# A fused RWKV-attention and squared-ReLU kernel: one written-out order of all work exchanged for another

## The chip, the cores and the metric

The kernel runs on one core of one Trainium2 chip. The metric is the device time of one execution in microseconds (us); lower is better. Five engines work side by side, each in its own order: PE (TensorE, matrix products), DVE (VectorE), ACT (ScalarE), POOL (GpSimd) and SP, which here only issues DMAs.

## What is computed

Four inputs r, k, v, w of shape 4 x 8 x 768 x 48 (batch, heads, time, head size) go through a recurrent attention with a state of 48 x 48 per head; its result y, laid out as 3072 tokens of 384, goes through a two-layer network with a squared ReLU.

```python
for t in range(S):
    cur = np.einsum('bhd,bhe->bhde', u[None] * kt, vt)
    y[:, :, t] = np.einsum('bhd,bhde->bhe', rt, state + cur)
    state = wt[:, :, :, None] * state + np.einsum('bhd,bhe->bhde', kt, vt)
x = y.transpose(0, 2, 1, 3).reshape(B * S, H * D)
h = x @ w_in            # 3072 x 384 @ 384 x 2048
r = np.maximum(h, 0.0)
return (r * r) @ w_out  # 2048 x 384
```

## The kernel before

The 3072 tokens are cut into 12 steps of 256 (4 batches of 3 steps). In a step two neighbouring times share a partition, so that every tile has 128 partitions. A step runs through these operations, each a small function named after its word in the order:

- Loads (`load_step`, L209): w, k, r, v of a step, 384 KB each. `load_wi` (L219) and `load_wo` (L224) load the two weights in four pieces of 768 KB into the staging tiles `w_st`; `cast` (L229) makes fp16 of them into `wi_sb` and `wo_sb`, on the engine that the word names.
- Decay: `ww_` (w·w, L295), `lw_` (its logarithm on ACT, L299), `cum_` (cumulative sums as products with triangular constants on PE, L337), `exp_` and `ac_` (ACT, L356 and L360), `rd_` (DVE, L369: r and k times their decay into `rdec_buf`).
- `tr_` and `rkt_` (L379, L387) transpose them on PE into `rkT_b` in the first three steps; later ones use a transposing DMA, `dtr_` (L392).
- `p_` (PE, L400) makes the scores, `pm_` (DVE, L413) masks them, `su_`, `ts_`, `sn_` (PE, mostly DVE, mostly POOL) carry the state S on.
- The term with u: `load_u` and `ub_` (L239, L243) spread the row u over all partitions with a product of PE, `uc_` copies it to `u_bc`; `ku_`, `qp_`, `q_`, `vq_` (L315 to L328) are k·u, its product with r, the sum of it over a head, and that times v.
- `y_`, `yq_`, `yc_`, `yb_`, `yd_` (PE, L465 to L502) add up y in a PSUM tile `att`; `ysb_` copies it as `y_sb_b`; `yt_` with `xt_`, or a transposing DMA `dyt_` (L527), turn it into `xT_b`.
- The network: `m1_` (L532) is one eighth of x @ w_in, six products of 128 x 256; `rl_` (relu, L541) and `sq_` (square, L549) make `gt_b`. `m2_` (L557) is a quarter of the second product for 128 tokens, four products; from step 5 on seven half-width products `pw_` (L601), with sums `tw_`, `sw_`, `cx_`, `ow_` around them, do its work. `store` (L637) writes the result.

`warm_` (L641) is a dummy: n products of 128 x 512 on a tile of zeros, whose result nobody reads. PE has two double tiles `att` and four single tiles `one`, which all of this takes in turns.

The order of everything is written out by hand in the table `ORDER` (L17 to L94): one word for each operation, in program order. A word names the operation, the step and the part; `:n` gives the PSUM tile, and `=A`, `=V` or `=G` the engine (ACT, DVE, POOL). A loop at L659 issues the words one after the other, so each engine gets its instructions in the order of the words that fall to it, and waits are placed where the data ask for them. Nothing reorders them later.

Of the kernel before, what the change touches and what calls it, by code (L numbers as in the profile page):

```python
# [22 lines left out]
tr_.1.0:0 y_.0:0 ld.2.k ld.2.r rkt_.1.1=V rkt_.1.0=V cast.i.0=A yq_.0 yc_.0 ysb_.0.0=V yd_.0 su_.1:1 ysb_.0.1=V
p_.1.1:m yt_.0.0:1 ku_.1=G sn_.0.1=G xt_.0.0=V yt_.0.1:0 qp_.1=G pm_.1.1 xt_.0.1=A cast.i.1=A p_.1.0:0 pm_.1.0
m1_.0.0:0 m1_.0.1:3 rl_.0.1=A rl_.0.0=A q_.1 ts_.1.0=V ww_.2=G sn_.1.0=G m1_.0.4:2 m1_.0.5:1 m1_.0.3:3 rl_.0.3=A
vq_.1=V lw_.2 rl_.0.5=V ts_.1.1=V m1_.0.2:0 ld.2.v y_.1:0 rl_.0.2=A cast.i.3=V ld.3.w yc_.1 yq_.1 yd_.1 ysb_.1=A
rl_.0.4=A ld.0.o ld.1.o cum_.2:1 m1_.0.7:0 exp_.2 rl_.0.7=A yt_.1:1 ku_.2=V ld.3.k rw_.2=G xt_.1=V m1_.0.6:2 kw_.2=V
sq_.0.0=V m1_.1.6:3 m1_.1.5:1 m1_.1.3:0 v_.2=A rl_.1.6=A rl_.1.5=A rl_.1.3=A m1_.1.0:3 rd_.2.0 ld.2.o ld.3.o rd_.2.1
rl_.0.6=V m1_.1.2:1 qp_.2=V m1_.1.1:0 sq_.0.1=A rl_.1.1=V rl_.1.2=A ac_.2 rl_.1.0=A ww_.3=G sq_.1.0=A m1_.1.7:2
tr_.2.0:1 cast.o.0=G su_.2:0 tr_.2.1:0 rkt_.2.0=V rkt_.2.1=V m1_.1.4:3 sn_.1.1=G ts_.2.0=V cast.o.1=G m2_.1.1.0:1  # L30
p_.2.0:0 ld.3.r p_.2.1:1 q_.2 pm_.2.0 rl_.1.4=A sn_.2.0=G vq_.2=G m2_.1.0.0:3 rl_.1.7=A m2_.0.0.0:2 m2_.0.1.0:0
pm_.2.1 m2_.0.1.1 m2_.0.0.1 ld.4.r yc_.2:1 yq_.2 cast.o.2=V kw_.3=V sq_.1.3=A ld.4.w sq_.0.3=A sq_.1.1=A lw_.3
cum_.3:0 sq_.0.2=A m2_.1.0.1 m2_.1.1.1 sq_.1.2=V ku_.3=V exp_.3 cast.o.3=A ld.4.k rw_.3=V m2_.0.0.2 m2_.0.1.2
m2_.1.1.2 m2_.1.0.2 m2_.0.1.3 qp_.3=V rd_.3.1 y_.2 ww_.4=G ld.3.v tw_.3=V rd_.3.0 yb_.2 m2_.1.1.3 m2_.0.0.3 os_.0.1=A
ysb_.2=A yt_.2:0 q_.3 m2_.1.0.3 lw_.4 dtr_.3.1 os_.1.1=A cum_.4:1 dtr_.3.0 xt_.2=V os_.0.0=A m1_.2.2:1 rw_.4=G
os_.1.0=A exp_.4 kw_.4=V ac_.4 ld.5.w rl_.2.2=A ku_.4=V qp_.4=G m1_.2.3:2 m1_.2.1:3 v_.3=A ac_.3 rl_.2.3=A rd_.4.1
vq_.3=G rl_.2.1=A rd_.4.0 ld.4.v m1_.2.0:0 ld.5.k ld.5.v m1_.2.6:1 rl_.2.0=V p_.3.0:0 ld.5.r rl_.2.6=A su_.3:1
# [663 lines left out]
```

## Time and profile before

| | us |
|---|---|
| three runs | 179.57, 179.72, 180.99; median 179.72 |
| profiled execution, its own time | 181.33 |
| its span, first to last instruction | 179.6 |
| busy: PE, DVE, ACT, POOL | 170.3, 150.6, 125.7, 113.9 |
| first product with w_in (L538) starts | 21.33 |
| last product of the result ends, about | 176.2 |

Times in rows of the profile are microseconds from the span's start, if not marked ns. A row of the timeline has start, duration, engine, line, operation, out<-in and how often (x8 are eight of them); what stands in brackets is how long the engine was idle just before, and what ended that wait. In a group of instructions stand, behind the bar, the busy time, the mean duration of one in ns, and the idle time before them. A busy share is an average over stages: what a change is worth is read from the stage and from the wait that ends last there. Matrix products are pipelined and overlap in the records, so eight of them in a row are better read by the time of all eight.

### The profile page before, as it was taken

The numbers are of one execution on the slowest core, as the hardware profiler recorded it, in microseconds if no ns is written. First come the engines' busy times: TensorE is split into PE (matmuls) and PEld (weight loads), VectorE is DVE, ScalarE is ACT, GpSimd is POOL, SyncE is SP. The second block draws the span as 40 slices with busy tenths as digits, with TensorE's granted clock in tenths as the row PEclk, the third lists the DMA queues.
The fourth block names the chain that finished last, engine by engine and source line by source line (L and its number), as shares of the span: only waits on it lengthen the run. The fifth ranks groups of instructions, "written<-read, shape, count | busy, mean of one in ns | idle before, by whom it ended". The sixth has DMA issues, their size and how long they took to land.

```text
span 179.6 us, 6485 instructions
## 1 busy us (share of the span) xinstructions
PE 170.3 (95%) x2771; PEld 134.3 (75%) x2771; DVE 150.6 (84%) x238; ACT 125.7 (70%) x209; POOL 113.9 (63%) x109
## 2 busy tenths in 40 slices
PE   7898799999999999998998999999999899999993
PEld 2274687856686777586875888888988788989992
DVE  5559899999689679999798999988899777768752
ACT  5368569897599667589675988688794777575510
POOL 6289944370575498155796399398989792392430
PEclk9999999999999999999999999999999999999999
DMA  5999999998999979799999959999989031040042
GB/s 153 324 353 377 350 253 350 271 309 229 228 260 243 268 192 236 151 303 133 275 185 300 227 130 262 135 183 271 235 221 157 4 91 36 12 175 0 4 173 92
DMA packets 82670, 36.59 MB, mean 204 GB/s; under 512 B 75857, under 2 KB 81106, under 8 KB 82642
## 3 DMA queue, kind: packets, MB, share of 16 engines
q1 hardware_dynamic: 82642, 36.19, 81.8%
q8 instruction: 21, 0.34, 0.8%
q14 instruction: 7, 0.06, 0.1%
HBM read 25.17 MB, written 4.72 MB: 166 GB/s over the span
## 4 chain that ended last, share of the span: by engine, by line
PE 79%; DVE 8%; DMA 5%; issue 3%; ACT 3%; DVEq 0%; ACTq 0%
PE one L538 31%; PE one L615 16%; PE one L561 12%; PE att L460 7%; DMA xT_b<-y_sb_b 3%; PE att L410 3%; PE att L433 2%; DMA w_b<-in_w_dram 2%; DVE pmT_b L421 2%; PE one L385 2%; PE one L643 1%; PE att L343 1%; ACT gt_b L545 1%; PE one L245 1%; ACT att L358 1%
## 5 line engine op out<-in xcount | busy, mean ns | idle before, releaser
L538 PE MATMUL one<-xT_b,wi_sb 128*128 128x256 bf16 x576 | 70.0, 273 | 1.3 <-ACT gt_b L545 0.7
L538 PEld LDWEIGHTS <-wi_sb 128*128 128x128 f16 x576 | 55.0, 98 | 10.0 <-issue 1.4
L545 ACT ACTIVATE gt_b<-one 128x512 f16<-128x512 f32 x71 | 41.0, 596 | 14.7 <-PE one L538 11.4
L553 ACT ACTIVATE gt_b<-gt_b 128x1024 bf16<-128x1024 f16 x39 | 40.3, 1052 | 1.7 <-DVE gt_b L547 1.4
L421 DVE TENSOR_TENSOR pmT_b<-att,mask 128x1024 bf16<-128x1024 f32 x22 | 26.7, 1219 | 3.0 <-PE att L410 2.8
L561 PE MATMUL one<-wo_sb,gt_b 128*128 128x384 f16 x160 | 28.7, 326 | 0.0
L615 PEld LDWEIGHTS <-gt_b 128*128 128x128 bf16 x280 | 23.3, 98 | 0.6
L561 PEld LDWEIGHTS <-gt_b 128*128 128x128 bf16 x160 | 15.0, 98 | 9.3
L547 DVE TENSOR_SCALAR gt_b<-one 128x512 f16<-128x512 f32 x25 | 16.9, 686 | 4.0 <-PE one L538 3.7
L321 POOL TENSOR_TENSOR ku_b<-ku_b,r_b 128x768 f32<-128x768 f32 x8 | 14.5, 1817 | 4.6 <-DVE ku_b L316 4.5
L327 POOL TENSOR_TENSOR vq_b<-v_b,q_b 128x768 bf16<-128x768 f32 x10 | 15.4, 1545 | 1.5 <-DVE q_b L324 0.9
L615 PE MATMUL one<-wo_sb,gt_b 128*128 128x192 f16 x168 | 16.3, 246 | 0.0
L447 POOL TENSOR_TENSOR S_b<-t_b,ac_buf 128x192 bf16<-128x192 f32 x17 | 9.2, 544 | 10.8 <-DVE t_b L443 7.1
L297 POOL TENSOR_TENSOR ww_b<-w_b 128x384 f32<-128x384 f32 x10 | 11.1, 1107 | 6.3 <-DMA w_b<-in_w_dram 6.3
L313 POOL TENSOR_TENSOR k_b<-k_b,w_b 128x384 f32<-128x384 f32 x8 | 9.1, 1132 | 7.6 <-DMA k_b<-in_k_dram 7.6
L316 POOL TENSOR_TENSOR ku_b<-k_b,u_bc 128x768 f32<-128x768 f32 x6 | 11.1, 1846 | 2.9 <-ACT u_bc L249 2.9
L510 ACT CAST y_sb_b<-att 128x768 bf16<-128x768 f32 x11 | 8.8, 799 | 5.3 <-PE att L460 4.8
L376 DVE TENSOR_TENSOR rdec_buf<-r_b,att 128x768 bf16<-128x768 f32 (+1 forms) x13 | 11.4, 886 | 0.9 <-ACT ac_buf L363 0.7
L376 DVE TENSOR_TENSOR rdec_buf<-k_b,att 128x768 bf16<-128x768 f32 (+1 forms) x13 | 11.5, 886 | 0.7 <-ACT ac_buf L363 0.3
L615 PE MATMUL one<-w_st_b,gt_b 128*128 128x192 f16 x112 | 11.4, 246 | 0.0
L324 DVE TENSOR_REDUCE q_b<-ku_b 128x16 f32<-128x768 f32 x12 | 11.3, 944 | 0.0
L358 ACT ACTIVATE att<-att 128x768 f32<-128x768 f32 x12 | 9.6, 801 | 2.1 <-PE att L345 1.9
(107 smaller groups left out, 287.1 us busy)
## 6 DMA issues: line engine op xcount, KB each, us to landing
w_b<-in_w_dram SPq DMA_DIRECT2D x12, 384.0 KB, 4.7
k_b<-in_k_dram SPq DMA_DIRECT2D x12, 384.0 KB, 4.9
r_b<-in_r_dram SPq DMA_DIRECT2D x12, 384.0 KB, 6.0
v_b<-in_v_dram SPq DMA_DIRECT2D x12, 384.0 KB, 4.8
out_dram<-w_st_b SPq DMA_DIRECT2D x23, 192.0 KB, 2.1
w_st_b<-in_moe_w_in_dram SPq DMA_DIRECT2D x4, 768.0 KB, 6.8
w_st_b<-in_moe_w_out_dram SPq DMA_DIRECT2D x4, 768.0 KB, 9.5
rkT_b<-rdec_buf SPq DMA_TRANSPOSE x18, 3.5
```

What stands on the lines that cost most here:

```text
L321: product("qp_", s)(ku[:], ku[:], buf("r", s)[:, :, 0:2, :])
L327: product("vq_", s)(buf("vq", s)[:].rearrange("p j h d -> p h j d"), buf("v", s)[:], buf("q", s)[:, :, :, None].to_broadcast([C, H, 2, D]))
L358: nc.scalar.activation(cs[:, :, 0:DM], cs[:, :, 0:DM], AF.Exp)
L376: nc.vector.tensor_mul(rdec[:, i, :, heads, 0:D], x.rearrange("p h j d -> p j h d"), decay[:, None, :, :].to_broadcast([C, 2, n, D]))
L421: nc.vector.tensor_mul(pmT, ps_p[:].rearrange("p e (a x) -> p (e a) x", a=2), mk.to_broadcast([C, 4, 2 * C]))
L460: nc.tensor.matmul(ps_y[rows, c, cols], lhsT, rhs, start=fresh, stop=True, skip_group_check=True)
L538: nc.tensor.matmul(ps1[:, j, :], wi_sb[:, n // 4, kk, n % 4 * 128:(n % 4 + 1) * 128], xT[:, :, kk, :], start=(kk == 0), stop=(kk == KT - 1))
L545: nc.scalar.activation(rl, m1, AF.Relu, scale=RS)
L547: nc.vector.tensor_scalar(out=rl, in0=m1, scalar1=RS, scalar2=0.0, op0=ALU.mult, op1=ALU.max)
L553: nc.scalar.activation(gt, rl, AF.Square)
L561: nc.tensor.matmul(m2, gt[:, n, c * C:(c + 1) * C], wo_sb[:, n, :], start=(n == 0), stop=(n == NT - 1))
L615: nc.tensor.matmul(where_to, gt[:, n, :], wo[:, n, :], start=(n == 0 and i in (1, 2, 5)), stop=(n == NT // 2 - 1), skip_group_check=True)
```

## The change

The table ORDER is exchanged for another one. The operations and functions stay; the words stand in another order, some name another engine or PSUM tile, and the dummies are other ones. Two lines of 77:

```diff
-ld.0.w ld.0.k ld.0.r ld.0.u ww_.0=V warm_.8.2 rw_.0=V ld.1.w lw_.0 cum_.0:1 exp_.0 ld.0.v ld.1.r ld.1.v ld.1.k ac_.0
+ld.0.w ld.0.k ld.0.v warm_.3.2 warm_.2.2 ld.0.r warm_.6.1 kw_.0=G ww_.0=V ld.0.u lw_.0 ld.1.w cum_.0:1 exp_.0
```

Where before eight dummies stood ahead of the first cumulative sums (`cum_.0`) and two ahead of the row u, now eleven and seven do; in all 26 instead of 21.

By count, some operations stand on other engines:

| operation | before | after |
|---|---|---|
| relu `rl_` | 71 ACT, 25 DVE | 78 ACT, 18 DVE |
| square `sq_` | 39 ACT, 9 DVE | 41 ACT, 7 DVE |
| r·w `rw_` and ku·r `qp_` | 16 POOL, 8 DVE | 20 POOL, 4 DVE |
| w·w `ww_` | 10 POOL, 2 DVE | 7 POOL, 5 DVE |
| state `sn_` | 17 POOL, 3 DVE | 15 POOL, 5 DVE |
| cast of w_in | 3 ACT, 1 DVE | 4 ACT |
| cast of w_out | 2 POOL, 1 DVE, 1 ACT | 4 POOL |
| v to bf16 `v_` | 8 ACT, 4 POOL | 8 ACT, 2 POOL, 2 DVE |
| second product's sums and copies `cx_`, `ow_`, `os_` | 24 ACT, 35 DVE | 26 ACT, 33 DVE |

On SP the loads at the program's start stood like this before (the numbers in the names are buffers; `w_b_68` holds step 0, `w_b_69` step 1):

```order
L212 DMA w_b_68<-in_w_dram 128x8x96
L212 DMA k_b_76<-in_k_dram 128x8x96
L212 DMA r_b_72<-in_r_dram 128x8x96
L240 DMA u_row<-in_u_dram 1x384
L212 DMA w_b_69<-in_w_dram 128x8x96
L212 DMA v_b_80<-in_v_dram 128x8x96
```

and now:

```order
L212 DMA w_b_68<-in_w_dram 128x8x96
L212 DMA k_b_76<-in_k_dram 128x8x96
L212 DMA v_b_80<-in_v_dram 128x8x96
L212 DMA r_b_72<-in_r_dram 128x8x96
L240 DMA u_row<-in_u_dram 1x384
L212 DMA w_b_69<-in_w_dram 128x8x96
```

v of step 0 moved ahead of r, the row u and w of step 1. Further on in SP's row, the four pieces of w_out stand directly behind the loads of step 2; before, w and k of step 3 stood ahead of and between them.

On DVE, from behind the first w·w up to the sum q of step 0 (`rdec_buf_140` and `rkT_b_100` are step 0, `pmT_b_102` its masked scores, `t_b` and `S_b` the state), before:

```order
L309 TENSOR_TENSOR r_b_72<-r_b_72,w_b_68 128x8x48
L376 TENSOR_TENSOR rdec_buf_140<-k_b_76,att_63 128x2x4x48
L376 TENSOR_TENSOR rdec_buf_140<-r_b_72,att_63 128x2x4x48 x2
L376 TENSOR_TENSOR rdec_buf_140<-k_b_76,att_63 128x2x4x48
L390 COPY rkT_b_100<-one_66 128x2x256
L390 COPY rkT_b_100<-one_64 128x2x256
L421 TENSOR_TENSOR pmT_b_102<-att_62,mask 128x1024
L418 TENSOR_TENSOR pmT_b_102<-one_64,mask 128x512
L418 TENSOR_TENSOR pmT_b_102<-one_65,mask 128x512
L324 TENSOR_REDUCE q_b_95<-ku_b_93 128x16
```

and now:

```order
L376 TENSOR_TENSOR rdec_buf_140<-k_b_76,att_63 128x2x4x48
L309 TENSOR_TENSOR r_b_72<-r_b_72,w_b_68 128x8x48
L376 TENSOR_TENSOR rdec_buf_140<-r_b_72,att_63 128x2x4x48
L376 TENSOR_TENSOR rdec_buf_140<-k_b_76,att_63 128x2x4x48
L376 TENSOR_TENSOR rdec_buf_140<-r_b_72,att_63 128x2x4x48
L390 COPY rkT_b_100<-one_65 128x2x256
L297 TENSOR_TENSOR ww_b_89<-w_b_69 128x384
L390 COPY rkT_b_100<-one_65 128x2x256
L421 TENSOR_TENSOR pmT_b_102<-att_62,mask 128x1024
L447 TENSOR_TENSOR S_b_106<-t_b_104,ac_buf_136 128x192
L443 TENSOR_TENSOR t_b_105<-S_b_106,att_63 128x192
L324 TENSOR_REDUCE q_b_95<-ku_b_93 128x16
```

r·w moved behind the first decay of k, w·w of step 1 came from POOL to between the copies, the first S product came from POOL, and q stands ahead of the second mask product instead of behind it.

On POOL, where w_out is cast (`w_st_b_84` to `87` are its four pieces, `vq_b_98` here that of step 2, `S_b` the state), before:

```order
L297 TENSOR_TENSOR ww_b_89<-w_b_71 128x384
L232 CAST wo_sb<-w_st_b_84 128x1536
L447 TENSOR_TENSOR S_b_109<-t_b_105,ac_buf_137 128x192
L232 CAST wo_sb<-w_st_b_85 128x1536
L447 TENSOR_TENSOR S_b_110<-t_b_104,ac_buf_138 128x192
L327 TENSOR_TENSOR vq_b_98<-v_b_82,q_b_97 128x8x2x48
L297 TENSOR_TENSOR ww_b_88<-w_b_68 128x384
```

and now:

```order
L305 CAST v_bf_b_92<-v_b_82 128x768
L321 TENSOR_TENSOR ku_b_93<-ku_b_93,r_b_74 128x768
L232 CAST wo_sb<-w_st_b_84 128x1536
L327 TENSOR_TENSOR vq_b_98<-v_b_82,q_b_97 128x8x2x48
L232 CAST wo_sb<-w_st_b_85 128x1536
L232 CAST wo_sb<-w_st_b_86 128x1536
L232 CAST wo_sb<-w_st_b_87 128x1536
L309 TENSOR_TENSOR r_b_75<-r_b_75,w_b_71 128x8x48
```

vq of step 2 moved from behind two casts to between the first and the second, and the two casts that DVE and ACT had are now behind it.

More of the change, by code (lines that the diff above doesn't have):

```diff
@@ L23 @@
[L23 to L37, printed above, removed]
@@ L93 @@
[L93 removed]
+ld.0.w ld.0.k ld.0.v warm_.3.2 warm_.2.2 ld.0.r warm_.6.1 kw_.0=G ww_.0=V ld.0.u lw_.0 ld.1.w cum_.0:1 exp_.0
+rd_.0.1.1 ld.1.r warm_.7.0 ld.1.k ub_:2 rw_.0=V ac_.0 ld.1.v uc_=A rd_.0.0.1 v_.0=A ku_.0=G rd_.0.1.0 tr_.0.0.1:3
+ld.0.i rkt_.0.0.1=A rd_.0.0.0 tr_.0.1.0:1 tr_.0.1.1:0 ld.1.i rkt_.0.1.0=V rkt_.0.1.1=A warm_.2.2 ww_.1=V tr_.0.0.0:1
+ld.2.i su_.0:1 qp_.0=G p_.0.1:0 ld.3.i rkt_.0.0.0=V ts_.0.0=A pm_.0.1 lw_.1 ld.2.w p_.0.0:n sn_.0.0=V ld.2.k cum_.1:0
@@ new lines @@
+ts_.0.1=V q_.0 ac_.1 yc_.0:1 yd_.0 warm_.5.2 kw_.1=G v_.1=A rw_.1=G pm_.0.0 exp_.1 vq_.0=G cast.i.0=A rd_.1.1 y_.0
+sn_.0.1=G yq_.0 rd_.1.0 tr_.1.1:2 ku_.1=G ysb_.0.0=A rkt_.1.1=V tr_.1.0:0 su_.1:0 rkt_.1.0=V cast.i.1=A yt_.0.0:1
+ysb_.0.1=V p_.1.1:m xt_.0.0=V ld.2.r yt_.0.1:0 pm_.1.1 qp_.1=G p_.1.0:1 xt_.0.1=A cast.i.2=A ld.2.v m1_.0.1:1
+ts_.1.0=V q_.1 m1_.0.2:2 sn_.1.0=G rl_.0.1=A m1_.0.0:0 pm_.1.0 vq_.1=G rl_.0.2=A m1_.0.4:1 ts_.1.1=V rl_.0.0=A
+m1_.0.5:2 y_.1:0 cast.i.3=A rl_.0.5=V yc_.1 yq_.1 ww_.2=G yd_.1 rl_.0.4=A ysb_.1=A ld.0.o ld.1.o m1_.0.3:0 m1_.0.6:3
@@ new lines @@
+ku_.2=V kw_.2=G lw_.2 ld.2.o rl_.0.3=A ld.3.o yt_.1:1 cum_.2:0 rl_.0.6=A xt_.1=V m1_.0.7:2 rw_.2=G sn_.1.1=G ld.3.w
+exp_.2 m1_.1.2:0 rl_.0.7=A v_.2=G rd_.2.1 m1_.1.6:1 rl_.1.2=A qp_.2=G m1_.1.1:3 rl_.1.6=V ac_.2 sq_.0.0=A tr_.2.1:0
+rd_.2.0 su_.2:1 rkt_.2.1=A m1_.1.0:2 ts_.2.0=V rl_.1.1=V ld.3.r ld.3.k m1_.1.3:1 cast.o.0=G rl_.1.0=A tr_.2.0:3
+rkt_.2.0=V m1_.1.4:2 m1_.1.5:0 rl_.1.3=A sn_.2.0=V q_.2 sq_.1.0=A sq_.0.1=A rl_.1.4=A sq_.0.3=A sq_.1.1=A rl_.1.5=V
+m2_.0.0.0:1 vq_.2=G p_.2.0:1 yc_.2:0 m1_.1.7:3 pm_.2.0 rl_.1.7=V cast.o.1=G m2_.1.1.0:0 m2_.1.0.0:2 yq_.2 sq_.1.2=A
@@ new lines @@
+sq_.0.2=A p_.2.1:1 cast.o.2=G m2_.0.1.0:3 pm_.2.1 m2_.0.1.1 m2_.0.0.1 cast.o.3=G ld.4.w ww_.3=V y_.2 ld.3.v tw_.1=V
+yb_.2 m2_.1.1.1 m2_.0.0.2 lw_.3 ld.4.k ku_.3=V cum_.3:1 m2_.0.0.3 exp_.3 kw_.3=V rw_.3=G os_.0.0=A ysb_.2=A ld.4.r
+m2_.1.0.1 qp_.3=G m2_.0.1.2 m2_.1.1.2 rd_.3.1 sq_.1.3=A rd_.3.0 yt_.2:1 ld.5.r xt_.2=A ww_.4=G m2_.0.1.3 m2_.1.1.3
+m1_.2.0:1 m2_.1.0.2 ld.5.w v_.3=V ac_.3 lw_.4 q_.3 os_.1.1=A dtr_.3.0 su_.3:0 rl_.2.0=A cum_.4:1 kw_.4=V ts_.3.0=V
+sn_.3.0=G m1_.2.5:0 exp_.4 os_.0.1=V m1_.2.1:1 rl_.2.5=A rw_.4=G rd_.4.1 m2_.1.0.3 rl_.2.1=A vq_.3=G m1_.2.7:0
@@ new lines @@
+m2_.3.0.2 m2_.3.1.3 ld.8.k cum_.6:1 ld.7.r rw_.6=G y_.5 exp_.6 yb_.5 m1_.4.2:2 m1_.4.0:0 ysb_.5=A ku_.7=G store.0.1
+rd_.6.1 os_.3.1=A dyt_.5 cum_.7:0 ac_.6 m1_.4.6:3 m2_.3.0.3 kw_.7=G rd_.6.0 q_.6 rl_.4.0=A rl_.4.2=A dtr_.6.1
+m1_.4.4:0 m1_.4.3:2 os_.3.0=V qp_.7=G ac_.7 exp_.7 rl_.4.6=A v_.6=A m1_.4.7:3 dtr_.6.0 rl_.4.4=V su_.6:1 rd_.7.1
+rl_.4.3=A tw_.4=V m1_.5.3:1 ld.8.w rl_.4.7=A sq_.4.3=A m1_.4.1:2 ld.7.v rl_.5.3=V m1_.5.7:0 ts_.6.0=A rw_.7=V ld.8.r
+rl_.4.1=A sn_.6.0=G m1_.4.5:3 rl_.5.7=A vq_.6=G ts_.6.1=V ld.9.w m1_.5.1:2 rd_.7.0 rl_.4.5=A p_.6.0:1 rl_.5.1=A
@@ new lines @@
+m1_.5.4:0 ku_.8=G pm_.6.0 store.1.0 sq_.4.2=A dtr_.7.0 m1_.5.6:2 yc_.6:0 rl_.5.4=V yq_.6 p_.6.1:1 ww_.8=G m1_.5.0:1
+rl_.5.6=A sq_.4.0=A pm_.6.1 m1_.5.5:3 v_.7=A sn_.6.1=G sq_.4.1=V rw_.8=G kw_.8=G y_.6 q_.7 dtr_.7.1 yb_.6 lw_.8
+su_.7:1 m2_.4.0.0:0 ts_.7.0=V rl_.5.5=A ysb_.6=A qp_.8=V dyt_.6 m2_.4.0.1 sn_.7.0=G sq_.5.2=A cum_.8:0 ni_.8=V
+sq_.5.3=A ts_.7.1=V ww_.9=G m1_.5.2:3 ld.8.v ac_.8 exp_.8 m2_.4.0.2 m2_.4.1.0:2 m2_.4.0.3 store.2.0 sw_.5.1.1=G
+rl_.5.0=A ld.9.r m2_.4.1.1 rd_.8.1 os_.4.0=A vq_.7=G ld.9.k p_.7.0:1 m2_.4.1.2 pm_.7.0 dtr_.8.1 m2_.4.1.3 rl_.5.2=A
@@ L94 @@
+pw_.11.7 ow_.9.3=A store.9.1 pw_.11.3 ow_.11.4=V pw_.11.4 store.11.1.1 ow_.11.2=V ow_.11.3=V store.11.0 warm_.1.5
+store.11.1.0
 """
```

105 lines of the change are left out of this document (45 added, 60 removed).

## The prediction

> **What bounds the kernel now.** I read the page first: the busy line of the engines and the granted clock of PE in 40 slices.
>
> ```profile
> span 179.6 us, 6485 instructions
> ...
> PE 170.3 (95%) x2771; PEld 134.3 (75%) x2771; DVE 150.6 (84%) x238; ACT 125.7 (70%) x209; POOL 113.9 (63%) x109
> ...
> PEclk9999999999999999999999999999999999999999
> ```
>
> PE is busy for 170.3 of 179.6 us, so all waits of PE together are 9.3 us. The products of the result are the same before and after the change, so it can win only waits, or lose by new ones. DVE is the next engine, at 84%.
>
> Next I asked who ends PE's idle time: the waits, engine PE (us in total, times, longest).
>
> ```profile
> PE one L643 <- DVE warm L267: 1.2, 1, 1.2
> PE one L385 <- DVE rdec_buf L376: 0.9, 2, 0.6
> PE att L341 <- ACT lw_buf L301: 0.7, 1, 0.7
> PE one L538 <- ACT gt_b L545: 0.7, 1, 0.7
> PE att L460 <- DVE y_sb_b L512: 0.7, 1, 0.7
> PE att L433 <- DVE pmT_b L421: 0.6, 1, 0.6
> PE att L410 <- DVE t_b L443: 0.6, 1, 0.6
> PE att L460 <- DVE t_b L443: 0.3, 1, 0.3
> PE one L538 <- DMA xT_b<-y_sb_b: 0.3, 1, 0.3
> PE one L538 <- ACT xT_b L525: 0.2, 1, 0.2
> ```
>
> These are all: 6.2 us. The warm, L385, L341, y_sb and xT rows (3.7 us) belong to the opening, before the first product with w_in. The other five (2.5 us) are scattered behind it; DVE ends three of them (1.5 us), ACT one (0.7), a DMA one (0.3).
>
> Then the opening itself, as a timeline (start, duration, engine, line).
>
> ```profile
> 1.19 3.59 PE L643 MATMUL one<-warm 128*128 128x512 bf16 x8 [1.19 <-DVE warm L267]
> ...
> 5.48 0.27 PE L341 MATMUL att<-half_ones,lw_buf 128*128 128x2 bf16 x4 [0.71 <-ACT lw_buf L301]
> ...
> 6.66 0.56 DVE L309 TENSOR_TENSOR r_b<-r_b,w_b 128x384 f32<-128x384 f32 x1 [1.85 <-DMA r_b<-in_r_dram]
> ...
> 7.20 1.64 PE L245 MATMUL one<-u_row,ones_row 1*128 1x384 f32 x2
> ...
> 8.88 0.48 ACT L249 COPY u_bc<-one 128x384 f32<-128x384 f32 x1 [1.42 <-PE one L245]
> ...
> 10.70 0.59 ACT L390 COPY rkT_b<-one 128x512 bf16<-128x512 bf16 x1 [0.27 <-PE one L385]
> ...
> 12.14 1.23 DVE L421 TENSOR_TENSOR pmT_b<-att,mask 128x1024 bf16<-128x1024 f32 x1
> ...
> 14.09 1.67 PE L643 MATMUL one<-warm 128*128 128x512 bf16 x7
> ...
> 20.63 0.36 DVE L525 COPY xT_b<-one 128x384 bf16<-128x384 bf16 x1 [0.28 <-PE one L520]
> ...
> 21.33 4.34 PE L538 MATMUL one<-xT_b,wi_sb 128*128 128x256 bf16 x36 [0.22 <-ACT xT_b L525]
> ```
>
> The first useful product with w_in starts at 21.33, when the first xT is there. The dummies tell PE's real speed: eight take 3.59 us at the start (0.45 each), seven take 1.67 us at 14 us (0.24 each). So PE runs at about half speed somewhere up to 14 us, though the page's granted clock reads 9 (90% or more) in every slice.
>
> **The change, part by part.**
>
> *Eleven dummies ahead, seven more behind the first cumulative sums.* Eleven at 0.45 us end at 1.19 + 4.9 = 6.1, where before the cumulative sums began at 5.48: 0.6 us late. The seven others come ahead of the row u. Before, the eight dummies were followed by 0.71 us of idle PE; now PE has work from 1.19 on without a gap. If that lifts the speed by about 7 us, the seven take 1.7 us, else 3.2, and the row u takes half of its 1.64, or all. With 0.9 us for the sums (5.48 to about 6.4 before) the row u ends at 6.1 + 0.9 + 1.7 + 0.8 to 1.64 = 9.5 to 10.3, against 7.20 + 1.64 = 8.84 before. The two rows bound the speed, 0.45 and 0.24 a dummy; I take the fast one from about 7 us on, since the idle gap that stood there is closed. The Trainium skill ("TensorE: Matmul & The Clock Gate", section "What's actually happening") says that the clock is halved until about 3.4 us of sustained work in a free-running window; by it the 3.59 us of before could miss a whole window, and the longer stretch cannot, so the sum by it would be the same. The two speeds in the rows agree with it.
>
> *v of step 0 third.* Two rows for what comes next:
>
> ```profile
> 4.24 1.15 SPq L212 DMA_DIRECT2D v_b<-in_v_dram  x1
> ```
> ```profile
> L305 ACT CAST v_bf_b<-v_b 128x768 bf16<-128x768 f32 x8 | 6.6, 828 | 0.0
> ```
> ```profile
> L512 DVE CAST y_sb_b<-att 128x384 bf16<-128x384 f32 x2 | 1.1, 558 | 0.6 <-PE att L460 0.6
> ```
>
> r of step 0 now starts behind v, which keeps SP for 1.15 us, so the product r·w moves from 6.66 to about 7.8. It ends at 8.4, ahead of the row u (9.5), and the decays and transposes that need it stand behind that row: it lies beside the dummies. In return ACT can cast v early, and does so ahead of its two copies of rkT: u copy 0.48 + v 0.83 + 2 x 0.59 = 2.5, so that the first mask product starts at 12.2 to 13.1 (PE's product between taking 0.2) instead of 12.14. From there to the end of the first xT DVE took 20.99 - 12.14 = 8.85 us. The new order puts the same DVE operations there, with one S product more (0.83, by its row below), one of the two y casts less (0.56, gone to ACT), and the casts' 0.6 us of waiting for PE gone, since y is complete before: 8.5. So the first xT ends at 20.7 to 21.6, 0.3 earlier to 0.6 later. I take +0.2, near the middle.
>
> *w_out loaded together and cast by POOL.* The casts and DVE's share:
>
> ```profile
> L232 POOL CAST wo_sb<-w_st_b x2: 1462/1462/1462, 34.2 to 36.3; 128x1536 f16<-128x1536 f32 x2
> ...
> L232 DVE CAST wo_sb<-w_st_b x1: 951/951/951, 39.5 to 39.5; 128x1536 f16<-128x1536 f32 x1
> ```
> ```profile
> 36.41 0.95 DVE L324 TENSOR_REDUCE q_b<-ku_b 128x16 f32<-128x768 f32 x1
> ```
> ```profile
> 38.16 1.47 POOL L327 TENSOR_TENSOR vq_b<-v_b,q_b 128x768 bf16<-128x768 f32 x1
> ```
> ```profile
> 37.15 3.42 PE L561 MATMUL one<-wo_sb,gt_b 128*128 128x384 f16 x20
> ```
>
> POOL's order is now: first cast, vq of step 2, then the other three casts without anything between. vq waits for q. With q at the time of before, vq ends at 37.4 + 1.5 = 38.9, the second cast at 40.4, the third at 41.8, the fourth at 43.3. On PE the second cast is needed by the fifth group of four products; five groups took 3.42 us from 37.15, so the fifth begins at 39.8. PE waits 0.6 at that place. If DVE's lighter load brings q 0.6 us earlier, the wait is nothing. Bounds 0 and 1.3 (vq as late as before, 39.6, + 1.46 = 41.1); I take +0.2, the nearer row being q's. The loads of step 3 that now queue behind w_out cost nothing: mask products of step 2 stand ahead of their first user on DVE. Without that cover the cumulative sum of step 3 would be late by what its w is.
>
> *Work moved between engines.* By count, DVE gives up 7 relus, 2 squares, 2 products each of ku·r and r·w and two casts, and takes 3 products w·w and 2 of S:
>
> ```profile
> L547 DVE TENSOR_SCALAR gt_b<-one 128x512 f16<-128x512 f32 x25 | 16.9, 686 | 4.0 <-PE one L538 3.7 <-ACT gt_b L545 0.2
> L555 DVE TENSOR_TENSOR gt_b<-gt_b 128x1024 bf16<-128x1024 f16 x9 | 6.6, 732 | 0.0
> L309 DVE TENSOR_TENSOR r_b<-r_b,w_b 128x384 f32<-128x384 f32 x4 | 3.9, 976 | 1.9 <-DMA r_b<-in_r_dram 1.9
> L321 DVE TENSOR_TENSOR ku_b<-ku_b,r_b 128x768 f32<-128x768 f32 x4 | 3.8, 951 | 0.0
> L447 DVE TENSOR_TENSOR S_b<-t_b,ac_buf 128x192 bf16<-128x192 f32 x3 | 2.5, 832 | 0.0
> ```
> ```profile
> L545 ACT ACTIVATE gt_b<-one 128x512 f16<-128x512 f32 x71 | 41.0, 596 | 14.7 <-PE one L538 11.4 <-PE one L615 2.0 <-DVE q_b L324 0.8
> L553 ACT ACTIVATE gt_b<-gt_b 128x1024 bf16<-128x1024 f16 x39 | 40.3, 1052 | 1.7 <-DVE gt_b L547 1.4
> ```
>
> DVE: -7 x 0.69 - 2 x 0.73 - 2 x 0.95 - 2 x 0.98 - 2 x 0.95 + 3 x 0.56 (r·w of the same shape at 6.66) + 2 x 0.83 = -8.7 us, to about 142 of 178 us. ACT: +7 x 0.60 + 2 x 1.05 = +6.3, to about 132. The two become alike, and neither comes near PE. Hence I let the 1.5 us that PE waits for DVE behind the opening go (bounds: nothing goes; all 2.5 us go), and keep ACT's 0.7 and the DMA's 0.3, since ACT gets more work and the number of transposing DMAs stays.
>
> *The end.* The last product groups, the dummy and the three last stores stand as before: 0.
>
> Sum: +0.2 + 0.2 - 1.5 = -1.1 us. The profiled execution took 181.33 us, 1.7 outside its span and 1.6 above the median of the runs (179.72); I make it 180.2, and put the same difference on the median: 178.6.
>
> **The rivals.**
>
> *All waits go.* The new order meets PE so well that all 2.5 us of late waits end, nothing is lost at the casts, and the opening is 0.3 us earlier: 179.7 - 2.8 = 176.9. For it: DVE's lighter load. Against: five waits with three different causes.
>
> *The waits only change places.* A wholly new order has its own late producers; 2.5 us of five small waits is about what any such order shows. Then 179.7, give or take 0.8. For it: the waits of before are on different lines, none repeated.
>
> *POOL's casts hold the second product (slower).* If q of step 2 is late, vq is, and three casts stand behind it on POOL, with four groups of PE behind each. The second cast ends 3.0 us after q, and PE wants it at 39.8: it decides from q's end at 36.8 on, and every us beyond costs one. q at 39.0 is a wait of 2.2 us, and with nothing won elsewhere 179.7 + 0.2 + 2.2 = 182.1. For it: POOL and DVE hold each other up.
>
> ```profile
> 93.31 2.24 DVE L309 TENSOR_TENSOR r_b<-r_b,w_b 128x384 f32<-128x384 f32 x1
> ```
> ```profile
> 93.32 1.81 POOL L321 TENSOR_TENSOR ku_b<-ku_b,r_b 128x768 f32<-128x768 f32 x1
> ```
>
> The product of 0.55 us took 2.24, beginning with a POOL product of 1.81. Two more POOL casts of 1.46 may so hold two DVE products, 2.9 us of DVE in all. The Trainium skill ("SBUF — State Buffer", section "SBUF: two separate sides") has the rule for it: DVE operations with two SBUF inputs and GpSimd's share a port under an exclusive lock; it speaks against this part, and the two rows agree.
>
> *The clock is not lifted by the dummies.* Then the seven take 3.2 us and the row u 1.64: it ends at 11.8, the first mask product starts near 14.5, 2.4 us late. With nothing won elsewhere that is 182.1. For it: eight dummies did not lift it before. Against: the idle 0.71 us is gone.
>
> **How the numbers follow.** The forecast has 0.40 (177.3 to 179.6), all waits gone (176.9) 0.20, places only changed (179.7) 0.20, POOL's casts 0.13, the clock 0.07 (both 182.1). About 1% (1.8 us) is what a measurement here tells from no change: faster is below 177.9, slower above 181.5. Faster: 0.20 and 0.3 of the forecast's 0.40, 0.32. Slower: 0.13 and 0.07, 0.20. Same: 0.48. The range leaves out part of the two slow cases and the best of the fast: 176.6 to 182.0.
>
> **What would show it.** Dummies ahead of the row u at 0.24 us or less; the first w_in product at 21 to 22 us; POOL's second w_out cast ended by 40.5 and no PE wait at L561; PE's waits on DVE behind 25 us under 0.5 in total; DVE busy near 142 us, ACT near 132. Wrong would be: dummies that stay at 0.45 up to the row u; one wait over 1.5 us at L561; waits on transposing DMAs or on ACT that add up to more than 2.5 us.

## The result, and the profile after

The new order took 178.53 us (median of 20 runs, 177.26 to 179.52), the old one beside it 180.06 us (20 runs, 178.35 to 182.35). The ratio is 0.9929, with a 95% interval of 0.9903 to 0.9954: 0.5 to 1.0% faster. That is a gain, but a smaller one than the 1% which the prediction took for the least that can be told from no change. The same new kernel, measured again later, gave 0.9876 (0.9831 to 0.9921). Ratios here and below leave out disturbed runs, which the quoted medians and ranges may hold; so the ratio decides wherever the two seem to differ.

The profiled execution took 178.68 us. Its page begins:

```profile
span 176.5 us, 6491 instructions
...
PE 168.2 (95%) x2774; PEld 133.3 (76%) x2776; DVE 142.8 (81%) x225; ACT 133.8 (76%) x223; POOL 114.8 (65%) x108
```

DVE has 142.8 us and ACT 133.8, close to the 142 and 132 of the forecast; POOL hardly changed. The span is 3.1 us shorter than in the profiled execution of before, but that one (181.33 us) was 1.3 us above the old kernel's median of 180.06: nearly half of the difference between the two profiles is luck, and a reading of the two traces must not explain more than 1.5 to 2 us of it.

The waits of the same execution, engine PE (us in total, times, longest):

```profile
PE att L341 <- DVE pmT_b L421: 1.5, 2, 0.8
PE one L643 <- DVE warm L267: 1.2, 1, 1.2
PE one L410 <- DVE rkT_b L390: 0.5, 1, 0.5
PE att L460 <- POOL vq_b L327: 0.4, 1, 0.4
PE one L385 <- DVE rdec_buf L376: 0.3, 1, 0.3
PE one L538 <- DVE w_st_b L634: 0.3, 1, 0.3
PE one L538 <- ACT xT_b L525: 0.2, 1, 0.2
PE att L460 <- DVE t_b L443: 0.2, 1, 0.2
PE one L643 <- issue: 0.2, 1, 0.2
```

Together 4.8 us, where it was 6.2. Only two waits lie behind the opening, the longer one of the first row (0.8, at 76 us) and the one on `w_st_b` (0.3, at 115 us): 1.1 us instead of 2.5. All five late waits of before are gone, ACT's and the DMA's too; both that remain are ended by DVE. That is one execution of each kernel. Other traces of the experiments below say the same: behind 25 us `b_11_7`, the old order with other dummies, has 2.2 us of such waits, while of the new order `a_again` has none, `a_casts` 0.7, `a_tw` 0.2 and `a_8` 1.2.

The opening, as a timeline:

```profile
1.19 4.88 PE L643 MATMUL one<-warm 128*128 128x512 bf16 x11 [1.19 <-DVE warm L267]
...
6.33 1.67 PE L643 MATMUL one<-warm 128*128 128x512 bf16 x7
7.94 0.91 PE L245 MATMUL one<-u_row,ones_row 1*128 1x384 f32 x2
...
20.56 3.44 PE L538 MATMUL one<-xT_b,wi_sb 128*128 128x256 bf16 x30 [0.22 <-ACT xT_b L525]
```

The eleven dummies take 0.45 us each as before, the seven 0.24, and the row u ends at 8.85, not at 9.5 to 10.3. The first product with w_in starts at 20.56, 0.77 earlier than in the profile of before (21.33). The last eight products of the result start there at 175.55 and here at 172.56:

```profile
172.56 0.82 PE L615 MATMUL one<-w_st_b,gt_b 128*128 128x192 f16 x8
```

So of the 3.0 us between the two traces 0.8 lie in the opening and 2.2 behind it. The late waits account for 1.4 of these 2.2; most of the rest is PE's busy time, which in this stretch fell from 151.6 to 150.9 us, and why it did is not shown. Nor can the 0.8 be put down to the new order: its opening stands unchanged in nine of the traces here, and the first product with w_in starts anywhere from 20.27 to 21.19 in them, while the old opening, at 21.33 above, has it at 20.25 in `h_open_before` below.

POOL's casts of w_out, DVE's sum q, and the second product beside them:

```profile
33.54 0.94 DVE L324 TENSOR_REDUCE q_b<-ku_b 128x16 f32<-128x768 f32 x1
```
```profile
34.63 1.47 POOL L327 TENSOR_TENSOR vq_b<-v_b,q_b 128x768 bf16<-128x768 f32 x1 [2.72 <-DVE q_b L324]
36.05 4.64 POOL L232 CAST wo_sb<-w_st_b 128x1536 f16<-128x1536 f32 x3
```
```profile
37.56 2.12 PE L561 MATMUL one<-wo_sb,gt_b 128*128 128x384 f16 x12
...
40.37 1.47 PE L561 MATMUL one<-wo_sb,gt_b 128*128 128x384 f16 x8
```

q starts at 33.54 instead of 36.41, since it stands earlier on DVE. vq and the casts follow at once, and the second cast has ended at about 37.5. The fifth group of four products, the first to need it, begins at about 38.2 (one group starts at 33.78, two at 35.66, and the fifth is the second of the row at 37.56), and no row of L561 carries a wait.

### The profile page after: what moved, and what is told of

Read it like the earlier page. It is cut to its first block, busy times and chain, and to the rows that moved or that the text cites. A ratio compares the mean times of both kernels' runs of the same rounds, so it can differ in the third digit from the quotient of the medians.

```text
span 176.5 us, 6491 instructions
## 1 busy us (share of the span) xinstructions
PE 168.2 (95%) x2774; PEld 133.3 (76%) x2776; DVE 142.8 (81%) x225; ACT 133.8 (76%) x223; POOL 114.8 (65%) x108
## 4 chain that ended last, share of the span: by engine, by line
PE 49%; DMA 3%; POOL 1%; SPq 1%; DVE 0%; issue 0%; DVEq 0%; POOLq 0%
PE one L538 22%; PE one L615 17%; PE att L460 4%; PE one L561 3%; DMA out_dram<-w_st_b 3%; PE att L410 2%; PE att L433 1%; SPq L212 1%; POOL gt_b L593 1%; PE att L343 1%; PE att L341 0%; POOL S_b L447 0%; DVE w_st_b L634 0%; DVE w_st_b L622 0%; PE att L345 0%
## 5 line engine op out<-in xcount | busy, mean ns | idle before, releaser
L545 ACT ACTIVATE gt_b<-one 128x512 f16<-128x512 f32 x78 | 45.2, 596 | 7.2 <-PE one L538 6.0
L553 ACT ACTIVATE gt_b<-gt_b 128x1024 bf16<-128x1024 f16 x41 | 41.9, 1053 | 0.2
L561 PE MATMUL one<-wo_sb,gt_b 128*128 128x384 f16 x160 | 29.4, 327 | 0.0
L321 POOL TENSOR_TENSOR ku_b<-ku_b,r_b 128x768 f32<-128x768 f32 x10 | 18.6, 1862 | 9.1 <-DVE ku_b L316 5.6
L561 PEld LDWEIGHTS <-gt_b 128*128 128x128 bf16 x160 | 14.8, 98 | 8.8 <-issue 0.2
L327 POOL TENSOR_TENSOR vq_b<-v_b,q_b 128x768 bf16<-128x768 f32 x10 | 14.8, 1484 | 6.7 <-DVE q_b L324 4.7
L447 POOL TENSOR_TENSOR S_b<-t_b,ac_buf 128x192 bf16<-128x192 f32 x15 | 8.7, 581 | 13.6 <-DVE t_b L443 6.2
L547 DVE TENSOR_SCALAR gt_b<-one 128x512 f16<-128x512 f32 x18 | 12.3, 685 | 3.1 <-PE one L538 3.1
L309 POOL TENSOR_TENSOR r_b<-r_b,w_b 128x384 f32<-128x384 f32 x10 | 11.2, 1122 | 0.1
L620 ACT ACTIVATE w_st_b<-one 128x192 f32<-128x192 f32 x14 | 4.5, 328 | 8.4 <-PE one L615 8.4
```

Source lines behind the costliest of these rows:

```text
L309: product("rw_", s)(r_raw[:, :, 2, :], r_raw[:, :, 1, :], w_raw[:, :, 0, :])
L321: product("qp_", s)(ku[:], ku[:], buf("r", s)[:, :, 0:2, :])
L327: product("vq_", s)(buf("vq", s)[:].rearrange("p j h d -> p h j d"), buf("v", s)[:], buf("q", s)[:, :, :, None].to_broadcast([C, H, 2, D]))
L545: nc.scalar.activation(rl, m1, AF.Relu, scale=RS)
L547: nc.vector.tensor_scalar(out=rl, in0=m1, scalar1=RS, scalar2=0.0, op0=ALU.mult, op1=ALU.max)
L553: nc.scalar.activation(gt, rl, AF.Square)
```

## The experiments

Theory L (load; theory A in the expectations): the late waits went because DVE has 8 us less to do. Theory D (dummies; rival B in the expectations, with the clock as its cause): the longer run of dummies lifts PE's speed earlier, and that is the gain. Theory F (fit): neither; which operation stands on which engine at which place decides, and the new table fits where its parts, taken one by one, do not. The expectations also name a rival C: the new arrangement brings the gain whichever engine has the operations that are moved. The kernels below change only words of ORDER; names such as `rl_.2.0` are relu, step, part.

### Halves of the two orders joined at the first product with w_in

`h_open_after` has the new order up to the first `m1_`, then what is left of the old one; `h_open_before` the reverse. (In `h_open_after` lines are numbered one lower.)

```diff
 h_open_after:  ... xt_.0.1=A cast.i.2=A ld.2.v
-m1_.0.1:1 ts_.1.0=V q_.1 ...
+pm_.1.0 m1_.0.0:0 m1_.0.1:3 rl_.0.1=A rl_.0.0=A q_.1 ...
 h_open_before: ... cast.i.1=A p_.1.0:0 pm_.1.0
-m1_.0.0:0 m1_.0.1:3 rl_.0.1=A rl_.0.0=A q_.1 ...
+ld.2.v m1_.0.1:1 ts_.1.0=V q_.1 ...
```

> The new order up to the first product with w_in, and from there the words of the old order, with the old engines. Theory A (the late waits that DVE's lighter load removes are the gain, the opening is even): the time of before, 180.1 us, 0.3 to either side, because the late part is the old one. Rival B (the opening is the gain: PE's speed doubles at 6 us instead of 14 and the first product with w_in starts 0.8 us earlier): 179.3 us, and its profile shows the first product with w_in at about 20.6 us. Where the two parts meet, a new wait could cost some tenths in either case.

> The old order up to the first product with w_in, and from there the words of the new order, with the new engines. Theory A: nearly the whole gain, 178.6 us. Rival B: no gain, about 180 us, 179.8 to 180.2. If both parts count, 179.2 to 179.4 us. The profile should show the first product with w_in at 21.3 us, as before.

Measured: `h_open_after` 180.69 us, ratio 1.0029 (0.9992 to 1.0066); `h_open_before` 180.06 us, ratio 0.9986 (0.9944 to 1.0027). Neither half has the gain. Each has a new wait at the seam, first `h_open_after`, then `h_open_before`:

```profile
26.02 0.57 PE L459 MATMUL att<-v_bf_b,pmT_b 64*128 64x48 bf16 x32 [0.89 <-DVE t_b L442]
```
```profile
20.25 0.82 PE L538 MATMUL one<-xT_b,wi_sb 128*128 128x256 bf16 x6 [0.22 <-ACT xT_b L525]
...
21.62 2.58 PE L538 MATMUL one<-xT_b,wi_sb 128*128 128x256 bf16 x22 [0.56 <-ACT wi_sb L232]
```

These 0.9 and 0.6 us come from the cut and are of the size of what is sought, so the split of the gain into opening and rest cannot be read from the medians. What the two do show: neither part brings its gain to the other order for nothing. Both starts of the first product with w_in also missed what was expected: 20.96 with the new opening, not 20.6, and 20.25 with the old one, not 21.3, although PE's granted clock reads 0.50 from 7.5 to 10.8 us in `h_open_before`. So this start wanders by about a microsecond under one and the same opening.

### The dummies alone

`b_11_7` is the old order with the counts of the new; `a_8` the new order with eight leading dummies (lines numbered one lower).

```diff
 b_11_7
-warm_.8.2 ... warm_.2.0
+warm_.11.2 ... warm_.7.0
 a_8
-ld.0.v warm_.3.2 warm_.2.2 ld.0.r warm_.6.1
+ld.0.v warm_.2.2 ld.0.r warm_.6.1
```

> The old order with one thing changed: eleven dummies instead of eight ahead of the first cumulative sums, seven instead of two ahead of the row u. Theory A: no gain, 180.1 us up to 180.6, since the dummies delay the first sums by 0.6 us. Rival B, with the clock as its cause: dummies behind 7 us take 0.24 us each, and the first product with w_in comes 0.3 to 0.8 us earlier: 179.3 to 179.8 us.

> The new order with three of the eleven leading dummies taken away, so that PE idles about 0.6 us ahead of the first cumulative sums as before. Theory A: no loss, 178.5 us, since the opening counts little. Rival B, with the clock as its cause: the speed stays low behind 7 us, the seven dummies take 3 us, the row u ends 1 to 2 us later, and the time rises to 179.3 to 180.5 us.

Measured: `b_11_7` 180.57 us, ratio 1.0001 (0.9963 to 1.0039); `a_8` 178.78 us, ratio 0.9928 (0.9879 to 0.9977). Theory D falls: the dummies bring nothing to the old order, and without three of them the new one keeps its gain. It is the dummies that are tested, not the speed: in the trace of `a_8` the speed rose early with eight dummies too (the last section has the rows), so what a late rise would cost the new order is not shown. The opening of `b_11_7`:

```profile
1.19 4.87 PE L643 MATMUL one<-warm 128*128 128x512 bf16 x11 [1.19 <-DVE warm L267]
...
6.60 1.89 PE L643 MATMUL one<-warm 128*128 128x512 bf16 x7
8.42 0.91 PE L245 MATMUL one<-u_row,ones_row 1*128 1x384 f32 x2
...
21.57 2.62 PE L538 MATMUL one<-xT_b,wi_sb 128*128 128x256 bf16 x21 [0.30 <-ACT xT_b L525]
```

The speed is lifted early here as well (the seven take 0.27 us each), and yet the row u, behind eight additional dummies, ends at 9.33 instead of 8.84, and the first product with w_in starts at 21.57: the early speed brings no earlier start here.

### Nine operations exchanged between DVE and ACT

`a_again` is the new kernel unchanged. `a_rl` gives nine operations that the new table has on ACT back to DVE; `b_rl` moves the same nine in the old order from DVE to ACT. The nine are a choice. The counts of seven relus and two squares in the table of the change are differences: word by word, 24 relus and squares went from DVE to ACT and 15 from ACT to DVE. So `a_rl` keeps every other engine of the new table.

```diff
 a_rl (new order)
-rl_.2.0=A rl_.2.5=A rl_.3.2=A sq_.3.1=A rl_.4.0=A rl_.5.6=A sq_.5.0=A rl_.6.3=A rl_.10.1=A
+rl_.2.0=V rl_.2.5=V rl_.3.2=V sq_.3.1=V rl_.4.0=V rl_.5.6=V sq_.5.0=V rl_.6.3=V rl_.10.1=V
 b_rl (old order): the same nine words, from =V to =A
```

> The new order unchanged, once more, beside the next three and on their chip. Every theory: 0.993 of before, within 0.4%. It is the yardstick for the three that follow, and a second look at the opening: if the first rise of PE's speed wanders from run to run, the first product with w_in starts somewhere between 20 and 21 us.

> The new order with seven relus and two squares given back from ACT to DVE, each in its place in the order; DVE has 6.3 us more work, ACT 6.3 us less, about their loads before the change. Theory A (DVE's lighter load is what removed the late waits): most of the 1.5 us comes back, 0.998 of before, 1.0 to 1.5 us above the new order. Rival C (the new arrangement does it, whatever engine has these nine): within 0.3 us of the new order.

> The old order with the same nine operations moved from DVE to ACT, each in its place. Theory A: 0.5 to 1.5 us below before, 0.992 to 0.997, since DVE ends three of the five late waits. Rival C: within 0.3 us of before, or above it, since ACT ended one wait already and gets 6.3 us more.

Measured, as ratios to the old kernel:

| | nine on DVE | nine on ACT |
|---|---|---|
| old order | 1 | 1.0164 (1.0084 to 1.0245) |
| new order | 1.0088 (1.0046 to 1.0130) | 0.9876 (0.9831 to 0.9921) |

Read across: the same move costs 1.6% in one order and gains 2.1 points in the other. Read down: the new order with these nine on DVE, and all its other engines, loses 0.9%; with the nine on ACT it gains. The two are no separate gains that add. Rival C wanted `a_rl` within 0.3 us of the new order, and falls. Theory L wanted `b_rl` faster, and in the new order a change of about the forecast's 1.5 us; it was slower, and in the new order 1.0088 - 0.9876 = 0.0212 of some 180 us, 3.8. The waits of `a_rl` behind the opening (the L341 row has one of 0.7 in the opening and one of 0.3 here):

```profile
PE att L410 <- DVE rdec_buf L376: 1.3, 1, 1.3
...
PE att L341 <- DVE pmT_b L421: 1.0, 2, 0.7
PE one L538 <- DVE gt_b L547: 0.7, 1, 0.7
PE one L615 <- DVE w_st_b L634: 0.7, 1, 0.7
PE one L561 <- ACT gt_b L545: 0.7, 1, 0.7
...
PE one L538 <- DVE w_st_b L634: 0.3, 1, 0.3
```

1.3 + 0.3 + 0.7 + 0.7 + 0.7 + 0.3 = 4.0 us. The trace of `a_again` has no such row behind the opening at all, so these waits are about the size of the whole loss. Which waits make the old order lose with the nine on ACT is not shown here; that part stays open.

### Load or place

Three kernels to part L from F. `a_swap` gives the nine to DVE and nine others to ACT, so that both engines keep the load of the new kernel. `a_rl_e` and `a_rl_l` give back the five early and the four late ones of the nine.

```diff
 a_swap (new order): the nine words of a_rl to =V, and
-rl_.1.7=V sq_.2.3=V rl_.3.6=V rl_.4.4=V rl_.5.3=V rl_.5.4=V sq_.4.1=V rl_.7.2=V rl_.9.1=V
+rl_.1.7=A sq_.2.3=A rl_.3.6=A rl_.4.4=A rl_.5.3=A rl_.5.4=A sq_.4.1=A rl_.7.2=A rl_.9.1=A
 a_rl_e (new order)
-rl_.2.0=A rl_.2.5=A rl_.3.2=A sq_.3.1=A rl_.4.0=A
+rl_.2.0=V rl_.2.5=V rl_.3.2=V sq_.3.1=V rl_.4.0=V
 a_rl_l (new order)
-rl_.5.6=A sq_.5.0=A rl_.6.3=A rl_.10.1=A
+rl_.5.6=V sq_.5.0=V rl_.6.3=V rl_.10.1=V
```

> The new order, with the nine relus and squares from ACT back on DVE, and nine others (seven relus, two squares, of steps 1 to 9) from DVE to ACT instead: by count both engines have what the new kernel gives them, DVE near 143 us and ACT near 134 us, only the places are others. If the load of the two engines makes the gain, the time stays that of the new kernel, ratio 0.985 to 0.996. If it is made by which operation stands on which engine at its place in the order, the time goes up by 2 us or more, ratio over 1.000, with late waits of PE on DVE and on ACT.

> The new order, only the five early ones of the nine (relus of steps 2, 3 and 4 and one square of step 3, 3.5 us of work) back on DVE. All nine cost about 4 us. If it is load, five parts of nine cost about 2.3 us and ratio is near 1.002. If it is one place, either this half or the other costs nearly all and the other nothing: ratio 0.99 or 1.01.

> The new order, only the four late ones (relus of steps 5, 6 and 10 and one square of step 5, 2.8 us of work) back on DVE. If it is load, about 1.8 us, ratio near 0.999. If it is one place, 0.99 or 1.01, the other way round than the early half. If both halves stay near 0.99, the 4 us come only when waits of the two halves meet.

Measured: `a_swap` 184.26 us, ratio 1.0231 (1.0182 to 1.0280); `a_rl_e` 179.79, 0.9990 (0.9959 to 1.0022); `a_rl_l` 180.25, 1.0001 (0.9965 to 1.0036). The page and the waits of `a_swap`:

```profile
PE 170.2 (93%) x2774; PEld 133.7 (73%) x2776; DVE 142.7 (78%) x225; ACT 132.9 (73%) x223; POOL 114.3 (63%) x108
```
```profile
PE one L538 <- ACT gt_b L545: 2.1, 3, 1.1
...
PE att L410 <- DVE rdec_buf L376: 1.1, 1, 1.1
PE att L341 <- DVE pmT_b L421: 1.0, 2, 0.7
...
PE one L538 <- DVE gt_b L547: 0.8, 1, 0.8
```

DVE and ACT do nearly as much work as in the new kernel (142.8 and 133.8 there), and the time is 3.0 to 3.6% longer, by which of the new kernel's two ratios is taken. Theory L falls with this line: the load of the two engines alone does not make the gain. PE's waits behind the opening add up to 4.5 us. ACT now keeps PE waiting too, 2.1 us. The longest of these waits, ACT's rows and then PE's:

```profile
137.29 2.00 ACT L553 ACTIVATE gt_b<-gt_b 128x1024 bf16<-128x1024 f16 x2
139.18 0.60 ACT L545 ACTIVATE gt_b<-one 128x512 f16<-128x512 f32 x1
```
```profile
139.83 0.81 PE L538 MATMUL one<-xT_b,wi_sb 128*128 128x256 bf16 x6 [1.10 <-ACT gt_b L545]
```

The relu at 139.18 is `rl_.9.1`, which the new table has on DVE; its word stands right behind two squares of ACT. On ACT it has to let both pass, 2.0 us, and PE waits 1.10 for the single tile that it empties.

Against the 0.9876 of `a_again` the halves cost 1.1 and 1.2 points, and all nine 2.1: the price does not sit at one place, it adds up. By itself this does not speak against load, for which 1.002 and 0.999 were expected and both intervals hold them; it is `a_swap` that parts load from place. One place can be followed to its end. In the new kernel DVE's row about 97 us is this:

```profile
96.44 1.23 DVE L421 TENSOR_TENSOR pmT_b<-att,mask 128x1024 bf16<-128x1024 f32 x1 [0.55 <-PE att L410]
97.58 0.95 DVE L376 TENSOR_TENSOR rdec_buf<-r_b,att 128x768 bf16<-128x768 f32 x1
```

and in `a_rl_l`, with the square `sq_.5.0` back on DVE, first DVE, then POOL, then PE:

```profile
96.46 1.22 DVE L421 TENSOR_TENSOR pmT_b<-att,mask 128x1024 bf16<-128x1024 f32 x1 [0.94 <-PE att L410]
97.60 1.34 DVE L555 TENSOR_TENSOR gt_b<-gt_b 128x1024 bf16<-128x1024 f16 x1
98.86 0.94 DVE L376 TENSOR_TENSOR rdec_buf<-r_b,att 128x768 bf16<-128x768 f32 x1
```
```profile
97.24 1.15 POOL L593 TENSOR_TENSOR w_st_b<-w_st_b,gt_b 128x512 bf16<-128x512 bf16 x1
```
```profile
99.85 0.42 PE L410 MATMUL att<-rkT_b 64*64 64x128 bf16 x16 [0.98 <-DVE rdec_buf L376]
```

The word `sq_.5.0` stands directly ahead of `rd_.8.0`. On DVE its 1.34 us push the decay of r from 97.58 to 98.86. That decay is the last to read a double tile `att` into which PE is to write the next scores, `p_.7.1`. PE did so at 98.69 in the new kernel, and now waits 0.98. So 0.98 of the square's 1.34 us reach PE. In the old order the same square was on DVE as well, but its word stood behind `rd_.8.0`, no wait of PE followed it, and it took half as long:

```profile
99.66 0.69 DVE L555 TENSOR_TENSOR gt_b<-gt_b 128x1024 bf16<-128x1024 f16 x1
```

In `a_rl_l` a product of POOL had begun 0.36 us ahead of the square and ran until 98.39. By estimate, a square of 0.69 would have left PE a wait of about 0.3. This is the fit, at one place: what stands behind the moved word, and what runs beside it on another engine. The other eight places were not followed in this way.

### Two parts by themselves: POOL's casts, and the wait at 76 us

`a_casts` gives the third cast of w_out back to DVE and the fourth to ACT. `a_tw` moves `tw_.3` on DVE behind the mask product that PE waited for at 76 us.

```diff
 a_casts (new order)
-cast.o.2=G ... cast.o.3=G
+cast.o.2=V ... cast.o.3=A
 a_tw (new order)
-tw_.3=V dyt_.4 yq_.5:0 ... pm_.5.1
+dyt_.4 yq_.5:0 ... pm_.5.1 tw_.3=V
```

> The new order, with the third cast of w_out on DVE and the fourth on ACT, as in the kernel before, instead of on POOL. If POOL's casts cost nothing, as the trace of the new kernel shows no wait at the second product, the time stays or rises a little by the 0.95 and 1.0 us that DVE and ACT get: ratio 0.988 to 0.998. If POOL's casts hold something up, by the port that DVE and POOL share, the time falls by 0.5 us or more: ratio under 0.987.

> The new order with one DVE operation moved: the third of the four differences of w_out, which took 2.54 us at 72.4 us beside POOL where the same kind takes 0.95 elsewhere, stands behind the second mask product of step 5 instead of ahead of it. PE's longest late wait, 0.8 us at 76.1 us for that mask product, should go: 0.5 to 0.9 us below the new order if that wait ends at a place on the path, nothing if another producer is late there too.

Measured: `a_casts` 178.04 us, ratio 0.9876 (0.9839 to 0.9913); `a_tw` 178.55 us, ratio 0.9914 (0.9876 to 0.9953). Neither parts from the new kernel's 0.9876 and 0.9929. The casts on POOL neither cost nor gain anything that can be measured, which with the two intervals means less than about 1 us. The wait at 76 us is not worth moving: in the trace of `a_tw` it is gone and the time is no lower, `a_casts` has it (0.7) and is no slower, and `a_again`, where nothing was moved, does not have it. The rows show why. In the profiled execution of the new kernel, POOL, then DVE and PE:

```profile
72.30 1.81 POOL L321 TENSOR_TENSOR ku_b<-ku_b,r_b 128x768 f32<-128x768 f32 x1 [3.32 <-DMA r_b<-in_r_dram]
```
```profile
72.38 2.54 DVE L580 TENSOR_TENSOR w_st_b<-wo_sb 128x1536 f16<-128x1536 f16 x1
74.85 1.21 DVE L421 TENSOR_TENSOR pmT_b<-att,mask 128x1024 bf16<-128x1024 f32 x1
```
```profile
76.11 0.24 PE L341 MATMUL att<-half_ones,lw_buf 128*128 128x2 bf16 x4 [0.82 <-DVE pmT_b L421]
```

and in `a_again`:

```profile
72.96 2.13 POOL L321 TENSOR_TENSOR ku_b<-ku_b,r_b 128x768 f32<-128x768 f32 x1 [3.89 <-DMA r_b<-in_r_dram]
```
```profile
72.47 0.95 DVE L580 TENSOR_TENSOR w_st_b<-wo_sb 128x1536 f16<-128x1536 f16 x1
73.45 1.22 DVE L421 TENSOR_TENSOR pmT_b<-att,mask 128x1024 bf16<-128x1024 f32 x1
```

If r's load lets POOL begin 0.08 us before DVE, DVE's product takes 2.54 us; if POOL begins 0.49 us behind, 0.95. In `a_casts` POOL began 0.25 us before it, and it took 2.38. A wait of 0.8 us of PE goes with which of the two comes first.

## Why the prediction was right in its total, step by step

The total was -1.1 us. The ratio of 0.9929 makes it -1.3, the two medians -1.5, and the second measurement -2.2. The time of 178.6 looks closer to 178.53 than the change was: it was counted from 179.72, the median of three runs, and the old kernel's median beside the new one was 0.34 higher. The terms, in the prediction's order:

- **Eleven and seven dummies, row u at 9.5 to 10.3: the working was too slow.** It let the sums behind the eleven take 0.9 us, at half speed. They took 0.5, because the speed was lifted at the end of the eleven, not at 7 us, and the row u ended at 8.85. The rival that the clock is not lifted at all falls with the same rows.
- **First xT 0.3 earlier to 0.6 later, taken +0.2: not confirmed, and its sign stays open.** The first product with w_in came at 20.56 (20.65 in `a_again`, 20.27 in `a_casts`), 0.7 to 1.1 earlier than in the one profile of before and outside the 21 to 22 that was to show it. But the start wanders by about a microsecond under either opening, and the old one had it at 20.25 once. How much of it the medians hold was not separated, since the joined halves have waits of their own.
- **Casts +0.2: mis-sized, it was 0.** The step took q at the time of before; q began 2.9 us earlier because its word had moved ahead in DVE's row. I had read that move for step 0, and did not look for it at step 2. `a_casts` agrees with the 0, to within about 1 us. The rival "POOL's casts hold the second product" falls, but with less room than its figure of 36.8 for q's end says. The sum counted the fifth group from the row at 37.15 and left out the one group that stood ahead of it in the old kernel, at 35.83; the fifth began at about 39.2 there, not 39.8. In the new kernel it began at about 38.2, so q had to end by about 35.2 and ended at 34.48.
- **Late waits -1.5: near in size, wrong in the reason.** They went from 2.5 to 1.1 us in the two profiles, -1.4, and the other traces of the new order have 0 to 1.2. But I let DVE's waits go because DVE's load would be lighter, and kept ACT's 0.7 and the DMA's 0.3. Those two went as well, and what remained hangs on DVE. The forecast "waits on DVE behind 25 us under 0.5 in total" failed, with 1.1. `a_swap` shows that the load alone was not the cause: with nearly the same busy time of both engines it was 2.3% slower than the old kernel.
- **End 0**: its waits show nothing new; PE has none behind 116 us.
- **Places only change** (179.7) was near to the mechanism, but not to the time: all of the old late waits went and new ones came, only fewer.
- **All waits go** (176.9): `a_again` has no late wait in its profile, and that execution still took 178.36 us. The lowest of the new kernel's runs is 177.26.

So the sum came near by luck in part: its one large term held its size by a wrong argument, and of the two small ones (the opening and the casts, together 0.4) one was 0 and the other stays open. Dividing PE's late waits by the engine that ended them, and letting one engine's share go with its load, did not describe what happened: where a wait could be followed, PE waited because two or three instructions stood in an unlucky sequence, on an engine that was busy for about 80% of the time.

## What to carry to other kernels

Where an order is written out, its engine assignments belong to it: nine small operations moved to the less busy engine gained 2.1 points in the order made for it and lost 1.6% in the other. Before forecasting a move, look at which instruction stands directly behind it on the engine it goes to and whether PE waits for that one; the busy share did not tell it here. And read a gain of 1% against several executions, since a single wait of 0.8 us came and went where one engine began 0.7 us later behind a DMA, and the first large product started up to a microsecond earlier or later with the same opening.

## What the runs showed of the hardware that was not expected

- **When PE's speed is lifted wanders from run to run, with the same instructions ahead.** Eleven leading dummies took 4.88 us in the new kernel; in `a_casts`, whose beginning is the same, they took 4.45, and in `a_rl_l` 3.87:

```profile
1.19 4.45 PE L643 MATMUL one<-warm 128*128 128x512 bf16 x11 [1.19 <-DVE warm L267]
```

  Eight took 3.59 us in the old kernel and 3.24 in `a_8`, where the row u behind them took 0.91 us (1.64 in the old kernel):

```profile
1.19 3.24 PE L642 MATMUL one<-warm 128*128 128x512 bf16 x8 [1.19 <-DVE warm L266]
...
7.40 0.91 PE L244 MATMUL one<-u_row,ones_row 1*128 1x384 f32 x2
```

  So eight leading dummies can be enough, and need not be. The Trainium skill ("TensorE: Matmul & The Clock Gate", section "What's actually happening") says that the window in which activity is counted runs freely and that the same kernel may meet it differently in each run; the rows agree with it.
- **How long a product of two SBUF tiles takes on DVE beside POOL differs from execution to execution**: 0.95 and 2.54 us for the same instruction in two executions of one kernel, above. The Trainium skill ("SBUF — State Buffer", section "SBUF: two separate sides") describes an exclusive lock that goes to whichever began first; both executions agree, DVE's being long where POOL began first, and POOL's (2.13 instead of 1.81 us) where DVE did.
